# Product 2 of the sequence transform, made once for both pairs of position blocks

## The chip, the core and the metric

The kernel runs on one core of a Trainium2 chip. Its time is device microseconds of that core; lower is better. The engines named below are TensorE (PE; PEld is its weight load), VectorE (DVE), ScalarE (ACT), GpSimd (POOL) and SyncE (SP); SyncE and GpSimd here only issue transfers.

## The reference

The reference mixes two branches of the same kind of input, with S = 2048 positions, D = 512 channels and F = 1792:

```
a = x @ Wd_re.T;  b = x @ Wd_im.T          # DFT along the channels
y = Cr @ a - Ci @ b                        # DFT along the positions, real part
h = relu(x' @ W_gate) * (x' @ W_up);  z = h @ W_down
g = sigmoid(sum(x * gate_w))               # one number per position
out = g * y + (1 - g) * z
```

Cr and Ci are 2048 x 2048 and are loaded from memory as they are used; nothing uses that they are cosines and sines. The change touches y.

## The kernel before, in words

**Products.** Every large product is made on TensorE from two-part numbers: an operand x is split into hi (a ScalarE copy to a shorter format) and lo (VectorE: x minus hi), and three matmuls lo*hi, hi*lo, hi*hi are added in a PSUM bank (PARTS). Every product of matrices is done in Strassen's manner, in Winograd's form: the two matrices are cut into 2 x 2 blocks, seven products of sums of blocks take the place of eight, and the result blocks are sums of these. In this form products 1 (A11*B11) and 2 (A12*B21) add up to result block 11, while the other six make the other three blocks together with product 1.

**Stages.** The hidden layer h (blocks, banks named c), the channel DFT (banks a), then six rounds with banks named z: two of class Down (h times W_down) and four of class Sequence, which make y. A result tile holds channels on the partitions and positions along the free dimension; out, zd have the layout (block of 512 positions, 128 partitions, 4 blocks of 128 channels, 512 positions).

**A round of y** (classes Round, line 779, and Sequence, line 901). A round belongs to one matrix (m = 0 for Cr, m = 1 for Ci) and one pair of 512-position blocks (p = 0 or 1); their order is (0,0), (0,1), (1,1), (1,0). Each of its seven products x has four steps jj, and a step has 2 result tiles x 2 pieces x 3 matmuls = 12 matmuls with 512 columns; so a product has 48 and a round 336. The moving operand (ch and cl, 128 x 1024 for a step) comes from blocks r11, r12, r22, r21 of Cr or Ci: loads by SyncE of 512 KB each (keyed 90 matmuls ahead of the product), sums on VectorE (40 ahead), hi on ScalarE (HI = 31 ahead) and lo on VectorE (LO = 24 ahead). The stationary operand (lh, ll for m = 0; lb, stored earlier and fetched again, for m = 1) is the split of a or b.

Products 1 and 2 go to one pair of banks A, 3 to E, 5 and 6 to B, 7 and 4 to D. After products 6, 2 and 4 the banks are read (evac, line 830): VectorE forms the result blocks 12, 22, 21 with the help of the copies u, n5 and w, and ScalarE copies 11. For m = 0 a result block is added to zd by an accumulating transfer, which GpSimd issues (done, line 962). For m = 1, zd is added to the block by an accumulating transfer, VectorE multiplies by g, and another accumulating transfer adds it to out. The last round has its own order (product 3 first), starts some banks from zd or out with ScalarE copies, and halves its very last step into two half banks (ze) of 256 columns, so that two engines can read and store them at the end.

**What sets the order.** The lines above do not issue instructions: they hand operations with a key (a position in the row of matmuls) to class Plan (line 129). Plan keeps TensorE's order by key and gives every other operation a due time, from which each engine's order follows. It takes an operation at the earliest 70 matmuls ahead of its key on VectorE and ScalarE (AHEAD 40 and FREE 30), 30 ahead on the queues of SyncE and GpSimd, and only when one of 51 working buffers of 4 KB a partition (UNITS) is to be had. The result is one fixed order for each engine; each engine carries out its own strictly in that order.

## Time and profile before

| what | us |
|---|---|
| median of 3 runs (lowest 794.5, highest 795.7) | 795.22 |
| the profiled execution, its own time | 794.13 |
| its span, first to last instruction | 792.4 |
| busy: PE, DVE, ACT, POOL | 787.1, 652.1, 332.6, 97.0 |
| granted TensorE clock, mean | 1.000 |

The profile shows one execution. Its span is 1.7 us shorter than the execution's time, since it counts from the first instruction to the last. A matmul is shown with its own length of some 389 ns, though the next one starts before it ends; so what a matmul costs is read from how many follow each other in a stretch without a gap, not from its mean. An entry such as `cl<-r,ch 128x1024` names what is written and what is read, with the size for 128 partitions; buffer numbers are left out. DMA rows give queue q1 (issued by SyncE), q0 (by GpSimd, the accumulating ones among them), with packets, MB and the share of the 16 DMA engines' time. An arrow in square brackets names what ended the wait in front of the instruction.

### The profile page before, as it was taken

How to read it: one execution, taken by the hardware profiler on the slowest of the kernel's cores; microseconds unless marked ns; L12 is line 12 of the kernel's file. 1: busy time of each engine (PE TensorE's matmuls, PEld its weight loads, DVE VectorE, ACT ScalarE, POOL GpSimd, SP SyncE). 2: the span in 40 equal slices, each digit the busy share in tenths (PEclk: the TensorE clock that was granted, in tenths of full speed). 3: DMA queues.
4: the chain of work that ended last, by engine and by line, in shares of the span. 5: the costliest groups of instructions: out<-in, count | busy, mean ns of one | idle time of the engine just before them, and what ended most of it. 6: DMA issues, size and time to landing. Idle time of an engine off the chain costs nothing.

```text
span 792.4 us, 9557 instructions
## 1 busy us (share of the span) xinstructions
PE 787.1 (99%) x3470; PEld 651.5 (82%) x3470; DVE 652.1 (82%) x778; ACT 332.6 (42%) x402; POOL 97.0 (12%) x151
## 2 busy tenths in 40 slices
PE   9999999999999999999999999999999999999997
PEld 7888888888888888888888888888888888888886
DVE  7999986868699466999886799997597549966996
ACT  5533221312133234274665668464343335442631
POOL 0101311111112122111121001001000100011001
PEclk9999999999999999999999999999999999999999
DMA  8614553232548599999899989217877994098766
GB/s 320 250 41 164 180 187 146 93 147 94 199 146 267 194 353 398 416 349 342 296 367 415 411 285 371 87 53 223 259 271 282 282 379 132 31 278 253 199 147 133
DMA packets 53888, 187.02 MB, mean 236 GB/s; under 512 B 6225, under 2 KB 6993, under 8 KB 53841
## 3 DMA queue, kind: packets, MB, share of 16 engines
q1 hardware_dynamic: 33680, 113.40, 39.9%
q0 software_dynamic: 20016, 72.89, 28.1%
q8 instruction: 27, 0.44, 0.2%
q14 instruction: 21, 0.16, 0.1%
q10 hardware_dynamic: 144, 0.13, 0.1%
HBM read 117.18 MB, written 69.21 MB: 235 GB/s over the span
## 4 chain that ended last, share of the span: by engine, by line
PE 99%; ACT 0%; DVE 0%; issue 0%
PE z L126 55%; PE c L126 34%; PE a L126 10%; PE warm L126 0%; PE ze L126 0%; ACT z L126 0%; DVE warm L126 0%
## 5 line engine op out<-in xcount | busy, mean ns | idle before, releaser
L126 ACT CAST ch<-r 128x1024 fp32r<-128x1024 f32 x112 | 116.0, 1052 | 132.4 <-DVE r L126 54.0
L126 PE MATMUL z<-cl,lh 128*128 128x512 f32 x420 | 163.4, 389 | 0.0
L126 PE MATMUL z<-ch,lh 128*128 128x512 f32 x420 | 163.4, 389 | 0.0
L126 PE MATMUL z<-ch,ll 128*128 128x512 f32 x420 | 163.4, 389 | 0.0
L126 DVE TENSOR_TENSOR cl<-r,ch 128x1024 fp32r<-128x1024 f32 x112 | 134.3, 1218 | 30.9 <-ACT ch L126 22.3
L126 PE MATMUL z<-ch,lb 128*128 128x512 f32 x444 | 136.8, 389 | 0.0
L126 PEld LDWEIGHTS z<-ch,lb 128*128 128x128 f32 x444 | 83.3, 188 | 17.3
L126 PEld LDWEIGHTS z<-cl,lh 128*128 128x128 f32 x420 | 78.8, 188 | 16.5
L126 PEld LDWEIGHTS z<-ch,lh 128*128 128x128 f32 x420 | 78.8, 188 | 16.3
L126 PEld LDWEIGHTS z<-ch,ll 128*128 128x128 f32 x420 | 78.8, 188 | 16.2
L126 PE MATMUL z<-cl,lb 128*128 128x512 f32 x222 | 86.4, 389 | 0.0
L126 DVE TENSOR_TENSOR r<-r,r 128x1024 f32<-128x1024 f32 x60 | 71.5, 1216 | 2.8 <-DMA r<-ci 2.5
L126 DVE TENSOR_TENSOR cl<-hr,ch 128x1024 fp32r<-128x1024 f32 (+1 forms) x56 | 59.8, 1085 | 13.2 <-ACT ch L126 11.3
L126 ACT CAST ch<-hr 128x1024 fp32r<-128x1024 f32 (+1 forms) x56 | 51.4, 942 | 27.7 <-DMA hr<-hd 13.2
L126 PEld LDWEIGHTS z<-cl,lb 128*128 128x128 f32 x222 | 41.7, 188 | 8.7
L126 ACT ACTIVATE g<-c 128x512 f32<-128x512 f32 x26 | 15.5, 597 | 62.7 <-PE c L126 62.5
L126 PE MATMUL c<-xl,wb0h 128*128 128x512 f32 x104 | 40.5, 389 | 0.0
L126 PE MATMUL c<-xh,wb0l 128*128 128x512 f32 x104 | 40.5, 389 | 0.0
L126 PE MATMUL c<-xh,wb1h 128*128 128x512 f32 x104 | 40.5, 389 | 0.0
L126 PE MATMUL c<-xh,wb0h 128*128 128x512 f32 x104 | 40.5, 389 | 0.0
L126 PE MATMUL c<-xh,wb1l 128*128 128x512 f32 x104 | 40.5, 389 | 0.0
L126 PE MATMUL c<-xl,wb1h 128*128 128x512 f32 x104 | 40.5, 389 | 0.0
(200 smaller groups left out, 1321.4 us busy)
## 6 DMA issues: line engine op xcount, KB each, us to landing
hr<-hd SPq DMA_DIRECT2D x42, 512.0 KB, 7.1
r<-cr SPq DMA_DIRECT2D x32, 512.0 KB, 4.8
r<-ci SPq DMA_DIRECT2D x32, 512.0 KB, 8.9
hd<-hs POOLq DMA_DIRECT2D x28, 512.0 KB, 4.7
lb<-lb SPq DMA_DIRECT2D x28, 512.0 KB, 4.7
ad<-a POOLq DMA_DIRECT2D x16, 512.0 KB, 6.0
l<-ad SPq DMA_DIRECT2D x16, 512.0 KB, 8.8
wr<-wgu SPq DMA_DIRECT2D x14, 512.0 KB, 6.5
```

The lines of the kernel that those rows point to most:

```text
L126: getattr(getattr(nc, self.engine), self.name)(*map(ap, self.a), **{k: ap(x) for k, x in self.k.items()})
```

## The change

Product 2 leaves the four rounds. Each round keeps six products in the order 1, 7, 6, 3, 5, 4 (288 matmuls), and result block 11 of a round is product 1 alone. After the two rounds of a matrix a new class Joint makes what is missing: A12 times B21 for both pairs p at once. With the two pairs side by side this is again a product of 2 x 2 blocks, and it is made by seven smaller products with 12 matmuls each (84 in all, one result tile for each bank). Its stationary operands jt are made in Joint.lefts from the stored ad, split, stored to a new place jb and fetched again; its moving operands jch and jcl come from four more blocks of Cr or Ci (jr). Its four result tiles are added to zd (m = 0) or gated and added to out (m = 1). The joint part of m = 1 is the last work of the kernel, and its last product is the one that is halved.

In the rounds the use of the banks changes: after product 1 ScalarE writes its negative into bank B, on which 6 and then 5 are added; after product 6 ScalarE copies the negative of B to u, VectorE subtracts D, and ScalarE starts bank G from u for product 4. Three of the four rounds add r21 to r11 by an accumulating load instead of a load and a VectorE sum. u is completed with zd for m = 1 before it goes into bank G, so block 21 needs no accumulating transfer after it. The keys of the fetches of lb and of the preparations of lefts[0] move with the new order.

The core of the diff, in its order:

```diff
     class Sequence(Round):
+        ORDER, NEW, FOUR = (1, 7, 6, 3, 5, 4), (1, 3, 7), "G"
         HI, LO = 31, 24
...
-                r = {b: buf(f"r{b}") for b in BLOCKS}
-                for b, key in (("11", at[1, jj]), ("22", at[3, jj]), ("12", at[5, jj]), ("21", at[2, jj] - 36)):
-                    op(key - 90, lambda r=r, b=b, jj=jj: load(r[b].all, source(b, jj)))
...
+                for b, x, t in (("11", 1, 90), ("12", 7, 110), ("22", 7, 105)):
+                    op(at[x, jj] - t, lambda r=r, b=b, jj=jj: load(r[b].all, source(b, jj)))
+                for x, o, a, b, sign in ((7, "12", "12", "22", 1), (6, "11", "11", "12", 1), (5, "12", "11", "22", -1)):
+                    op(at[x, jj] - 40, lambda r=r, o=o, a=a, b=b, sign=sign: combine(r[o].all, r[a].all, r[b].all, sign))
+                if self.fourth:
+                    op(at[5, jj] - 36, lambda r=r, jj=jj: accumulate(r["11"].all, source("21", jj)))
+                else:
+                    r["21"] = buf("r21")
+                    op(at[4, jj] - 90, lambda r=r, jj=jj: load(r["21"].all, source("21", jj)))
+                    op(at[4, jj] - 40, lambda r=r: combine(r["11"].all, r["11"].all, r["21"].all, 1))
...
+            def seed():
+                b.new()
+                for n in range(2):
+                    minus(b[n], a[n])
+            def seed4():
+                g.new()
+                for n in range(2):
+                    copy(g[n], u[:, n])
+            if x == 1:
+                op(key, seed)
+                op(key + 1, lambda: both(copy, o["11"], a))
+                self.done("11", key + 6)
+            elif x == 6:
+                op(key, lambda: both(minus, u, b))
+                op(key + 1, lambda: [E().vector.tensor_sub(u[:, n], u[:, n], d[n]) for n in range(2)])
+                if self.m:
+                    op(key + 6, lambda: accumulate(u.all, zd[self.place("21")]))
+                op(key + 50, seed4)
+            elif x == 5:
+                o["12"] = w
+                op(key, lambda: both(copy, w, b))
+                op(key + 1, lambda: both(E().vector.tensor_add, o["22"], d, w))
...
+    class Joint:
+        ORDER = (1, 7, 6, 5, 2, 4, 3)
+        def __init__(self, m, last=False):
+            self.m, self.last, self.base, self.lead = m, last, plan.now, 130 if last else 85
...
+                for p in range(2):
+                    op(self.base - 60, lambda p=p: load(self.v[p].all, out[2 * p, :, 0:2]))
+            for x in self.ORDER:
+                t = self.t[x] = buf(f"jt{x}", [2, 4, P], F32R)
+                op(self.at[x, 0] - 60, lambda t=t, x=x: load(f32(t.all), jb[m, x - 1]))
...
+                if last and x == 3:
+                    for h in range(2):
+                        pe(6, self.halves, h)
+                else:
+                    for jj in range(2):
+                        pe(6, self.product, x, jj)
+                    self.evac(x, plan.now)
...
+        def rights(self, jj):
+            r = {b: buf(f"jr{b}") for b in BLOCKS}
+            at = {x: self.at[x, jj] - self.lead for x in self.ORDER}
...
+            for b, x in (("11", 1), ("12", 1), ("22", 7), ("21", 2)):
+                op(at[x] - 60, lambda b=b: load(r[b].all, source(b)))
...
+                if x == 4:
+                    op(at[6] + 6, lambda: accumulate(r["11"].all, source("21")))
+                if self.last and x == 3:
+                    g = self.g[:, 1].unsqueeze(1).to_broadcast([P, 2, N])
+                    op(at[x] - 3, lambda o=o, g=g: E().vector.tensor_mul(r[o].all, r[o].all, g))
+                hi, lo = self.c[x, jj] = [buf(f"jc{y}{x}", dtype=F32R) for y in "hl"]
+                op(at[x], lambda hi=hi, o=o: E().scalar.copy(hi.all, r[o].all))
+                op(at[x] + 5, lambda hi=hi, lo=lo, o=o: E().vector.tensor_sub(lo.all, r[o].all, f32(hi.all)))
...
+            def seed():
+                self.new("X")
+                e.scalar.activation(bank("X"), bank("A"), AF.Copy, scale=-1.0)
+            def seed3():
+                e.vector.tensor_add(s, bank("B"), s)
+                e.vector.tensor_mul(s, s, self.g[:, 1])
+                e.vector.tensor_add(s, s, self.v[1][:, 0])
+                for n, h in enumerate(HALVES):
+                    self.new(f"H{n}")
+                    e.scalar.copy(self.b[f"H{n}"][:, h], s[:, h])
+            def done(p, n):
+                f = o[p][:, n]
+                e.vector.tensor_mul(f, f, self.g[:, p])
+                e.vector.tensor_add(f, f, self.v[p][:, n])
+                load(out[2 * p, :, n], f)
...
+            if x == 1:
+                op(key, seed)
+            elif x == 6:
+                op(key, lambda: e.scalar.copy(s, bank("X")))
+                op(key + 1, lambda: e.vector.tensor_add(y, bank("D"), s))
...
+    plan.rest = 150
+    for m, k in ((0, 60), (1, 800)):
+        Joint.lefts(m, plan.now + k, 10)
+    plan.rest = plan.REST
     for n, (m, p) in enumerate(((0, 0), (0, 1), (1, 1), (1, 0))):
         if n == 1:
-            for i, x in enumerate(ORDER_Z):
+            for x, key in zip(Sequence.ORDER, (60, 110, 340, 390, 440, 490)):
                 for k in range(2):
-                    lefts[1].fetch(x, k, plan.now + 48 * i + 24 * k + 40, lb)
-        Sequence(lefts[m], m, p, n == 3)
+                    lefts[1].fetch(x, k, plan.now + key + 24 * k, lb)
+        Sequence(lefts[m], m, p, n != 2)
+        if n % 2:
+            Joint(m, m == 1)
```

More of the change, by code (lines that the diff above doesn't have):

```diff
@@ L103, in __init__ @@
             self.reads += self.writes
-        self.after, self.start, self.end, self.due = set(), None, None, None
+        self.after, self.start, self.end, self.due, self.rest = set(), None, None, None, None
         n = writes[0].size() if self.writes else 0
@@ L356, in __getitem__ @@
             return self.banks[n].all
-        def part(self, n, columns):
-            return self.banks[n][:, columns]
     def E():
@@ L796, in __init__ @@
             for x in self.ORDER:
-                self.seed(x, plan.now)
-                self.products(x)
+                for jj, n in enumerate(counts):
+                    pe(6 * n, self.product, x, jj)
                 self.evac(x, plan.now)
@@ L1015, in end @@
[L1015 to L1025 removed]
+            g = self.g[:, int(b[1]) - 1].unsqueeze(1).to_broadcast([P, 2, N])
```

272 lines of the change are left out of this document (141 added, 131 removed).

## The prediction

> **What bounds the kernel now.** I read the chain of work that ended last first. Its rows give start, length and what ran.
>
> ```profile
> 4.49 231.45 PE c L126 x1020
> 235.94 76.16 PE a L126 x336
> 312.10 38.08 PE c L126 x168
> 350.18 436.56 PE z L126 x1926
> 786.74 1.44 PE ze L126 x12
> 788.18 0.02 issue
> 788.20 0.37 ACT z L126
> ```
>
> From 4.49 to 788.18 us the end is set by TensorE alone, with no wait in it. 436.56 us over 1926 matmuls is 0.2267 us for one with 512 columns; 1.44 us over 12 is 0.120 us for one with 256. So time is the number of matmuls, as long as every operand is there in time. The four rounds of y are the last 1344 of these products (1338 with z and 512 columns, 6 split into the 12 of ze): they end at 788.18, and the last one begins 330 x 0.2267 + 1.44 = 76.25 us earlier, at 711.93.
>
> Next, the four rounds one by one (window, PE, PEld, DVE, ACT and POOL busy, clock, DMA share, GB/s), to see what stands close behind TensorE.
>
> ```profile
> 483.40:559.60 76.20, 76.20 (x338) 63.11 (x337) 67.86 (x64) 38.27 (x42) 3.64 (x5) 1.00 0.52 167
> 559.60:635.80 76.20, 76.20 (x338) 63.11 (x337) 55.32 (x52) 30.19 (x33) 3.36 (x4) 1.00 0.84 277
> 635.80:711.90 76.10, 76.10 (x337) 63.01 (x337) 59.84 (x56) 33.48 (x37) 5.16 (x6) 1.00 0.61 199
> 711.90:788.20 76.30, 76.27 (x343) 63.20 (x341) 66.53 (x62) 28.47 (x32) 8.54 (x10) 1.00 0.73 187
> ```
>
> VectorE is busy 55 to 68 of 76 us, the DMA engines 0.52 to 0.84 of the time, ScalarE less than half. The clock is 1.00 throughout. VectorE and the DMA engines are the two to watch.
>
> Third, how far VectorE stands ahead of TensorE, and what eats that lead. These are VectorE's rows around the start of the last round.
>
> ```profile
> 696.15 3.51 DVE L126 TENSOR_TENSOR cl<-r,ch 128x1024 fp32r<-128x1024 f32 x3
> ...
> 721.85 1.23 DVE L126 TENSOR_TENSOR cl<-r,ch 128x1024 fp32r<-128x1024 f32 x1 [2.34 <-ACT ch L126]
> 724.63 1.22 DVE L126 TENSOR_TENSOR r<-r,r 128x1024 f32<-128x1024 f32 x1 [1.55 <-DMA r<-ci]
> 726.79 1.22 DVE L126 TENSOR_TENSOR r<-r,r 128x1024 f32<-128x1024 f32 x1 [0.94 <-DMA r<-ci]
> 727.93 2.48 DVE L126 TENSOR_TENSOR cl<-r,ch 128x1024 fp32r<-128x1024 f32 x2
> ```
>
> By the order of its instructions, the third cl of the first row belongs to the last round's first product: it is done at 699.66, and needed at 711.93, a lead of 12.3 us. The first cl of the last row belongs to the round's third product: done at 727.93 + 1.22 = 729.15, needed 96 matmuls into the round, at 733.69, a lead of 4.5 us. In 30 us VectorE lost 7.8 us, and two of its waits name loads. The DMA rows of that stretch, 696 to 730 us, say why:
>
> ```profile
> q0 software_dynamic: 957, 3.46, 51.0%
> q1 hardware_dynamic: 1843, 6.70, 50.9%
> ```
>
> Both queues together fill all 16 engines for 34 us. So before has no stall, but in its densest 34 us of transfers it used up most of its cover.
>
> **The change part by part.** *Matmuls.* Each round loses one of seven products: 4 x 48 = 192 go. Each of the two joint parts has 7 products x 2 x 6 = 84, so 168 come. Net 24 fewer; and the halved last product makes 24 half matmuls of 12 full ones, where before made 12 of 6. Full matmuls of y: 1338 before, 1152 + 156 = 1308 after, so 30 x 0.2267 = 6.80 us go and 12 x 0.120 = 1.44 us come. **The gain on the path is 5.36 us**, certain as long as nothing waits.
>
> *VectorE.* Its prices, from the trace: one operation, and three in a row.
>
> ```profile
> L126 DVE TENSOR_TENSOR cl<-r,ch 128x1024 fp32r<-128x1024 f32 x112 | 134.3, 1218 | 30.9 <-ACT ch L126 22.3
> 653.47 3.49 DVE L126 TENSOR_TENSOR r<-r,r 128x1024 f32<-128x1024 f32 x3
> 775.51 1.28 DVE L126 TENSOR_TENSOR z<-z,w 128x512 f32<-128x512 f32 x2
> ```
>
> An operation on 1024 columns lasts 1.22 us, but three take 3.49, so the next begins after 1.135 us; on 512 columns after 0.60 (1.28 for two of 0.69). A joint part needs 6 sums and 14 cl, 20 operations on 1024 columns, for 84 matmuls. In the changed order of VectorE, from the fourth round's first cl to the sum that waits for the joint part's product 5, stand 64 operations on 1024 columns and 9 on 512: 64 x 1.135 + 9 x 0.60 = 78.0 us, for 288 + 48 matmuls = 76.2 us. Up to the first cl of product 4, 240 matmuls into that round, it is 48 and 4: 56.9 us and 1.2 for the operation itself, against 54.4 us. VectorE then has no spare time and loses 3.7 us of lead by work alone. The waits that before's last round shows in front of its first dozen operations (2.34, 1.55 and 0.94 us above) are 4.8 us more if they come again. 8.5 us are asked of a lead that was 12.3 at the start of a round and 4.5 at its thinnest: the outcome lies between 3.8 us to spare and 4.0 us late. The nearest row for the state at that point is neither end, since the transfers below are denser than before's; I take **1.8 us late**.
>
> *Transfers.* Prices from the 34 us above, in units of 0.524 MB: accumulating, 0.51 x 34 / (3.46 / 0.524) = 2.62 us; plain, 0.509 x 34 / (6.70 / 0.524) = 1.35 us. From the first load of the first joint part to the end, the changed queues issue 88 plain units (78 full loads and 6 gate rows of half a unit on SyncE, 7 stores of jb on GpSimd) and 29 accumulating ones: 88 x 1.35 + 29 x 2.62 = 195 us. The matmuls of the two joint parts and of rounds three and four last 84 + 288 + 288 full ones and 72 full with 24 half: 149.6 + 19.2 = 168.8 us. The first of these loads are keyed 85 + 60 matmuls ahead, 33 us, so some 192 us stand open (the last 10 us take only results), but the second round's 4 accumulating loads, 10 us, fall into that stretch too. By these prices the engines are 195 + 10 - 192 = 13 us short. A shortage shows first as a loss of VectorE's lead, and the same lead pays for VectorE's own 3.7 us: of 8 to 12 us some 4.3 to 8.6 are left for the transfers, and 4.4 to 8.7 us could reach TensorE. The best that the trace shows is a slice of before with 434 GB/s, 1.21 us for a unit:
>
> ```profile
> GB/s 265 279 275 275 279 270 279 352 410 419 424 410 231 236 284 289 275 275 260 289 289 265 270 260 294 424 270 279 265 265 308 260 279 251 304 410 434 366 313 111
> ```
>
> At that price, with 2.42 for an accumulating one, it is 177 + 10 us: nothing is short. So this part costs 0 to some 9 us. I take **0.7 us** besides the 1.8, near the lower end, because before lived through 34 full microseconds without a stall. The Trainium skill, DMA: Bandwidth & Descriptors, Specifications, gives about 358 GB/s as the limit of HBM for one core. By that rule the 117 units, with the 29 read a second time, would take 146 x 0.524 / 0.358 = 214 us by estimate, and the change would lose some 19 us more than at the prices above; the slices above 400 GB/s here contradict it.
>
> *Banks filled by ScalarE.* Banks X (for product 6 of a joint part) and B are begun with ScalarE copies, and TensorE waits for them. In a round a whole product of 48 matmuls, 10.9 us, lies between; in a joint part only product 7, 12 matmuls, 2.7 us, against one copy of 0.58 us:
>
> ```profile
> L126 ACT COPY u<-z 128x512 f32<-128x512 f32 x8 | 4.6, 584 | 6.1 <-PE z L126 6.1
> z<-zd POOLq DMA_DIRECT2D x5, 512.0 KB, 8.2
> r<-ci POOLq DMA_DIRECT2D x4, 512.0 KB, 9.0
> ```
>
> Queued ahead of that copy on ScalarE is a ch that waits for an accumulating load (9.0 us to landing in the last row). Bounds: nothing, or the 2 to 3 us by which such a ch could be late. I put nothing extra, since it is late only where VectorE is late already.
>
> *The last product.* Its half banks need sums of VectorE after product 5: two of 512 columns, one gating of 1024 that stands between, two more of 512, then a ScalarE copy: 4 x 0.60 + 1.135 + 0.58 = 4.1 us, under products 2 and 4, 24 matmuls, 5.4 us. That holds by 1.3 us, unless the gating waits for its accumulated operand (8.2 us to landing). After product 5 VectorE has 13 operations, 12 x 0.60 + 1.135 = 8.3 us, against 5.44 + 24 x 0.120 = 8.3 us of matmuls: between nothing and half a microsecond of tail, **0.3 us** taken. The rest of the tail (copy, store, 4.2 us from the last matmul to the span's end) keeps its form.
>
> *Sum.* -5.36 + 1.8 + 0.7 + 0.3 = -2.6 us. The profiled execution took 794.13 us (span 792.4 and 1.7 around it), so 791.5; the median of the runs shown, 795.22, lies 1.1 above it: **792.6 us**.
>
> **The rivals.**
> 1. *Nothing waits.* All cover holds, as it does in before, where not one of 3450 matmuls waits. 795.22 - 5.36 = 789.9 us. Against it: VectorE at 78.0 of 76.2 us, where before has 66.5 of 76.3.
> 2. *The transfers become the bound* (the other side). 29 accumulating units where before's last two rounds issue some 16, and 14 stores and loads of jb for each joint part that before has not. It decides from the point where the shortage less the lead that is left exceeds 5.36 us, that is, when a transfer costs the 1.35 and 2.62 us throughout; at the 8.7 us above: 795.22 - 5.36 + 8.7 = 798.6 us. For it: two queues at 102% over 34 us already. Against it: that stretch still cost no matmul.
> 3. *VectorE's lateness just eats the gain*: the 4.0 us end of its bound with 1 to 2 us from the banks of the joint part, 795 us, within 0.2% of before.
> 4. That the change does not do what it says is excluded: the changed program has 3452 matmuls, 24 of them half, for 3470 with 12.
>
> **How the numbers follow.** A measurement of this kernel can tell about 0.2%, 1.6 us, from no change, so faster means under 793.6 and slower over 796.8. Forecast (1 to 3.8 us lost) 0.42, rival 1 0.18, rival 3 0.16, rival 2 0.24. Faster 0.60, same 0.16, slower 0.24. The range starts at rival 1 with the scatter of the runs (lowest 794.5, 0.7 under the median), 789.2, and reaches just past rival 2's time, to 799.0; I leave some 0.06 below and 0.12 above.
>
> **What would show it.** Right: 24 fewer full-width matmuls' time in z and j together, short waits of TensorE on cl near the third product or later of the fourth round, VectorE busy over nine tenths of the last 80 us, a DMA share near 1.0 in the third round. Wrong: no wait of TensorE at all (then the cover was underrated), or waits on loads already in the third round that add up to over 5 us (then the transfers decide), or waits of product 6 of a joint part on ScalarE. What I could have wrong above all is the lead at the start of the fourth round, which I took from before.

## The result, and the profile after

The changed kernel takes **803.77 us** (median; 803.62 to 804.83) beside 794.97 us of the kernel before in the same runs: 1.0113 times as long, with a 95% interval of 1.0095 to 1.013. The forecast was 792.6 us, and its range ended at 799.0. The profiled execution took 803.78 us.

The page of the changed kernel, its span and its engines (busy time, share, instructions):

```profile
span 802.0 us, 9737 instructions
...
PE 787.2 (98%) x3452; PEld 646.7 (81%) x3452; DVE 671.8 (84%) x810; ACT 361.0 (45%) x452; POOL 118.8 (15%) x180
```

There are 3452 matmuls, as the change says. A busy time of 787.2 us for fewer matmuls than before means nothing, since a matmul that waits in the pipeline is shown longer. What counts is the distance from one start to the next. The chain of work that ended last, in order of time (start, length, what ran; the largest pieces of the last six rounds and the joint parts):

```profile
350.81 133.50 PE z L126 x589
...
532.46 14.91 DMA r<-cr
...
549.80 35.27 PE z L126 x155
585.07 15.47 DMA jr<-cr
...
618.08 2.79 PE z L126 x11
...
625.90 15.60 DMA r<-ci
641.51 15.12 DMA r<-ci
...
660.35 27.27 PE z L126 x119
...
695.87 21.33 DMA r<-ci
...
761.55 10.57 DMA jr<-ci
...
794.57 2.88 PE jH L126 x24
```

Up to 484 us the chain is TensorE without a break, as before. Then it leaves TensorE several times, and each time it goes back to a transfer of 11 to 21 us: in the first round, in the second, about the end of the first joint part, at the end of the third round and in the fourth. The same by stage (window, busy PE, PEld, DVE, ACT and POOL, clock, DMA share, GB/s); the windows are the first round, the second, the first joint part, the third round, the fourth, and the last joint part:

```profile
483.90:552.50 68.60, 66.28 (x290) 53.93 (x289) 59.73 (x62) 38.27 (x47) 11.04 (x16) 1.00 0.75 240
552.50:620.70 68.20, 66.43 (x289) 53.71 (x288) 56.53 (x53) 39.10 (x46) 8.47 (x10) 1.00 0.89 260
620.70:639.70 19.00, 19.00 (x85) 15.76 (x84) 13.84 (x14) 6.83 (x10) 1.70 (x2) 1.00 1.01 315
639.70:706.50 66.80, 65.89 (x290) 54.00 (x290) 58.58 (x60) 33.68 (x42) 8.94 (x13) 1.00 1.04 373
706.50:778.10 71.60, 67.38 (x290) 53.58 (x289) 64.13 (x59) 39.26 (x45) 11.12 (x13) 1.00 0.97 268
778.10:797.40 19.30, 19.30 (x97) 16.33 (x95) 17.73 (x23) 5.14 (x8) 3.41 (x4) 1.00 0.92 193
```

A round is 288 matmuls, 288 x 0.2267 = 65.3 us. So the rounds stand still for 3.3, 2.9, 1.5 and 6.3 us, 14.0 together, and the joint parts (84 x 0.2267 = 19.0 us for the first) not at all. With 5.36 us gained, 0.6 us more ahead of the first round and 0.4 us of tail, the span should grow by 9.6 us: it went from 792.4 to 802.0.

The waits that the profile names for TensorE (us in total, times, the longest) do not say transfers:

```profile
PE z L126 <- DVE cl L126: 7.0, 12, 1.8
PE z L126 <- ACT ch L126: 2.1, 2, 1.5
```

They are the last link only. One step further back stand loads. The transfers of 30 us around the start of the fourth round (690 to 720 us; queue, packets, MB, share; then what was issued, how often, KB, and the median us to landing):

```profile
q1 hardware_dynamic: 1791, 6.52, 54.3%
q0 software_dynamic: 1198, 4.31, 48.7%
...
r<-ci SPq DMA_DIRECT2D x10, 512.0 KB, 19.5
```

In the kernel before, the 34 us around the start of its fourth round (696 to 730 us) had 50.9 and 51.0%, and looked the same by that number. But a full share cannot show how much stands in line behind it. The time to landing can: 19.5 us here, and half of that before:

```profile
r<-ci SPq DMA_DIRECT2D x10, 512.0 KB, 9.8
```

VectorE's rows around that place in the changed kernel (start, length, operation, and in brackets its idle time in front):

```profile
700.49 1.22 DVE L126 TENSOR_TENSOR cl<-r,ch 128x1024 fp32r<-128x1024 f32 x1
...
710.68 2.36 DVE L126 TENSOR_TENSOR cl<-r,ch 128x1024 fp32r<-128x1024 f32 x2 [2.15 <-ACT ch L126]
717.29 2.36 DVE L126 TENSOR_TENSOR r<-r,r 128x1024 f32<-128x1024 f32 x2 [4.25 <-DMA r<-ci]
719.69 1.23 DVE L126 TENSOR_TENSOR cl<-r,ch 128x1024 fp32r<-128x1024 f32 x1
```

By the order of instructions the first row is the fourth round's first cl, done at 701.71 and needed at 706.7: a lead of 5.0 us, where before had 12.3. VectorE then idles 4.25 us for a load, and the cl of the last row is done at 720.92, just when TensorE, which has waited 0.5 us for it, goes on. That load (the chain's row of 695.87) was not issued late, as it would be if no buffer had been free: its key is 105 to 110 matmuls, 24 to 25 us, ahead of a step that without a wait begins at 720.1 us, so it was due at 695 to 696 us.

The first round's stall has a queue in it. GpSimd's rows (start, length, how many transfers were issued, its idle time in front), and TensorE's behind them:

```profile
529.55 1.10 POOL L126 DMA_DIRECT2D jb<-jt  x2 [7.89 <-ACT ch L126]
530.64 0.92 POOL L126 DMA_DIRECT2D r<-cr  x1
531.92 0.55 POOL L126 DMA_DIRECT2D jb<-jt  x1 [0.36 <-issue]
532.46 0.90 POOL L126 DMA_DIRECT2D r<-cr  x1
```

```profile
548.54 0.49 PE L126 MATMUL z<-ch,ll 128*128 128x512 f32 x1 [1.54 <-ACT ch L126]
549.80 0.50 PE L126 MATMUL z<-cl,lh 128*128 128x512 f32 x1 [0.77 <-DVE cl L126]
```

The accumulating loads of r21 (r<-cr) stand behind stores of jb on GpSimd, which carries out its queue in order and had idled 7.89 us before them. The last one is issued at 532.46 and lands 14.91 us later, at 547.4, and then ch, cl and TensorE follow in turn.

### The profile page after: what moved, and what is told of

Its sections match the earlier page's. It is cut to its first block, busy times and chain, and to the rows that moved or that the text cites. A ratio compares the mean times of both kernels' runs of the same rounds, so it can differ in the third digit from the quotient of the medians.

```text
span 802.0 us, 9737 instructions
## 1 busy us (share of the span) xinstructions
PE 787.2 (98%) x3452; PEld 646.7 (81%) x3452; DVE 671.8 (84%) x810; ACT 361.0 (45%) x452; POOL 118.8 (15%) x180
## 4 chain that ended last, share of the span: by engine, by line
PE 75%; DMA 12%; DVE 8%; issue 3%; ACT 1%; POOL 0%; DVEq 0%; ACTq 0%; POOLq 0%
PE c L126 34%; PE z L126 29%; PE a L126 9%; DMA r<-ci 6%; DVE cl L126 3%; DMA jr<-cr 2%; DMA r<-cr 2%; DVE r L126 2%; DMA jr<-ci 1%; DVE jr L126 1%; PE jA L126 1%; ACT ch L126 1%; DVE jcl L126 1%; PE jD L126 1%; DVE jt L126 0%
## 5 line engine op out<-in xcount | busy, mean ns | idle before, releaser
L126 PE MATMUL z<-cl,lh 128*128 128x512 f32 x388 | 151.7, 391 | 2.6 <-DVE cl L126 2.5
L126 PE MATMUL z<-ch,ll 128*128 128x512 f32 x388 | 151.1, 389 | 1.5 <-ACT ch L126 1.5
L126 PE MATMUL z<-ch,lh 128*128 128x512 f32 x388 | 151.0, 389 | 0.0
L126 ACT CAST ch<-r 128x1024 fp32r<-128x1024 f32 x96 | 98.1, 1049 | 84.9 <-DVE r L126 50.5
L126 DVE TENSOR_TENSOR cl<-r,ch 128x1024 fp32r<-128x1024 f32 x96 | 115.4, 1221 | 22.7 <-ACT ch L126 22.4
L126 PE MATMUL z<-ch,lb 128*128 128x512 f32 x384 | 119.1, 390 | 0.7 <-ACT ch L126 0.5
L126 PEld LDWEIGHTS z<-ch,lb 128*128 128x128 f32 x384 | 72.1, 188 | 16.4 <-ACT ch L126 1.5
L126 PEld LDWEIGHTS z<-ch,lh 128*128 128x128 f32 x388 | 72.8, 188 | 14.9
L126 PE MATMUL z<-cl,lb 128*128 128x512 f32 x192 | 75.5, 393 | 4.5 <-DVE cl L126 4.5
L126 DVE TENSOR_TENSOR r<-r,r 128x1024 f32<-128x1024 f32 x52 | 62.5, 1220 | 8.8 <-DMA r<-ci 8.8
L126 ACT ACTIVATE g<-c 128x512 f32<-128x512 f32 x26 | 15.5, 597 | 65.8 <-PE c L126 65.8
L126 POOL DMA_DIRECT2D hd<-h x28 | 17.7, 634 | 174.4 <-DVE h L126 174.2
## 6 DMA issues: line engine op xcount, KB each, us to landing
r<-ci SPq DMA_DIRECT2D x28, 512.0 KB, 14.3
```

What stands on the lines that cost most here:

```text
L126: getattr(getattr(nc, self.engine), self.name)(*map(ap, self.a), **{k: ap(x) for k, x in self.k.items()})
```

## The theories

**A: transfers.** The DMA engines have a backlog, loads land late, and what VectorE and TensorE show is the consequence. **B: VectorE.** It has too much work, and the loads would have done. A third reading, **C**, is that a single link is at fault, such as the accumulating load of r21 ahead of product 4. Each has a run or more that takes its own cause away from the changed kernel, and each of A and B one that adds its own cause to the kernel before. The runs named thin_, and no_joint, leave parts of the result out; they show times only.

The table is worked out from the trace of each run: from the first matmul of a stage to the first of the next, less its matmuls at 0.2267 us. So it is the time that TensorE stood still (or ran slower) in that stage. The stalls are those of the one profiled execution, the time in the last column is the median; where a kernel's executions differ much, the two do not belong together (the profiled one of alternate took 795.9 us, of thin_results 795.7, of direct_early_plain 794.5).

| run | round 1 | round 2 | joint 1 | round 3 | round 4 | time, us |
|---|---|---|---|---|---|---|
| the changed kernel | 3.3 | 2.9 | 0 | 1.5 | 6.3 | 803.8 |
| thin_results | 2.1 | 3.0 | 0.1 | 0 | 0 | 796.7 |
| thin_sums | 0 | 0 | 0 | 0.5 | 4.3 | 795.4 |
| thin_both | 0.1 | 0 | 0 | 0 | 0 | 790.5 |
| plain_fourth | 1.1 | 0 | 0 | 2.3 | 8.8 | 805.3 |
| thin_r21 | 0.3 | 0 | 0 | 0 | 6.7 | 797.1 |
| thin_jb | 0.2 | 1.9 | 0 | 0 | 0 | 792.5 |
| thin_lefts | 0 | 2.0 | 0 | 1.5 | 5.6 | 800.1 |
| no_joint | 0.3 | 0 | - | 0 | 0 | 762.8 |
| before_extra1 | 11.6 | 15.1 | - | 24.1 | 12.8 | 861.9 |
| before_extra_half | 3.1 | 1.2 | - | 10.3 | 6.7 | 816.9 |
| before_again | 0.7 | 0 | - | 0 | 9.4 | 804.9 |
| direct_early | 1.6 | 4.6 | 0 | 0 | 0.2 | 796.8 |
| direct_early_plain | 0.4 | 1.0 | 0 | 1.4 | 0 | 793.3 |
| late_fetch | 0 | 0 | 1.9 | 0 | 0 | 793.6 |
| late_fetch_100 | 0 | 1.0 | 0 | 0 | 0 | 792.3 |
| alternate | 0 | 5.1 | 0 | 0 | 0.2 | 798.2 |

The last joint part stood still in none of them.

## The experiments

### Less of one thing in the changed kernel

**thin_results.** In the method that carries an instruction out:

```diff
+        def cut(x):
+            return ap(x)[:, 0:1, 0:128] if isinstance(x, Ref) else x
...
+        f = cut if "accum_op" in self.k and names & {"zd", "out"} else ap
```

> The changed kernel with every instruction in its place; only the accumulating transfers that touch zd or out carry 128 of 1024 columns each, so seven eighths of those sums are left out of the result. Theory A (the DMA engines are full, loads land late, and all other lateness follows): some 28 transfers at 2.62 us become 0.3 us each, over 60 us of engine time go in the four rounds, r<-ci lands in under 10 us again (14.3 in the changed kernel), the stalls of TensorE at the ends of the third round and in the fourth round's product 7 (1.5 and 4.5 us) vanish, and the time comes to 791 to 796 us. Theory B (VectorE's own amount of work is what is late): its 84% stay, the stalls stay, the time stays within 2 us of 803.8.

Measured: 796.72 us (794.83 to 799.72), 1.0023 times before (1.0008 to 1.0039). The waits of TensorE that are left:

```profile
PE z L131 <- DVE cl L131: 2.5, 5, 0.8
...
PE z L131 <- ACT ch L131: 0.7, 1, 0.7
```

r<-ci lands in 9.5 us in place of 14.3, and the third and the fourth round have no stall at all, although VectorE does exactly what it did. There it is the transfers. The stalls of the first and the second round stay (2.1 and 3.0 us, before 3.3 and 2.9), so the result transfers are not their main cause.

**thin_sums.** The same method, with another condition: `f = cut if self.name in ("tensor_add", "tensor_sub") and names <= {r11, r12, r21, r22 and the same with jr} else ap`.

> The changed kernel with every instruction in its place; VectorE's sums of the blocks of Cr and Ci (r and jr) are made on 128 of 1024 columns, so the rest of those sums is left out of the result. Over 50 sums at 1.135 us become some 0.2 us, so VectorE's busy time falls from 671.8 us to about 615 to 620. Theory B (VectorE's own work is the limit): the stalls go, 790 to 793 us. Theory A (loads land late): the wait for the loads is the same, though VectorE makes up for it faster; the stalls that begin with a late load remain, at the least the two at the ends of the first and third rounds and most of product 7 of the fourth, together 6 us or more, 797 to 803 us.

Measured: 795.42 us (793.81 to 797.43), 1.0005 times before (0.9995 to 1.0015). This lies between what the two theories gave, and below what A allowed. The stretch 698.8 to 768.4 us, its fourth round:

```profile
698.80:768.40 69.60, 66.29 (x290) 53.79 (x289) 49.28 (x60) 38.76 (x45) 11.11 (x13) 1.00 1.00 279
```

VectorE is busy 49 of 69.6 us and TensorE still stands for 4.3 us; r<-ci lands in 14.3 us as before. But the first two rounds have no stall, and the others less. A VectorE with time to spare makes good a late load. So A is right on where the stalls of the last two rounds start, and wrong in that VectorE would not matter: its work alone makes the difference between 14.0 and 4.8 us of stalls.

**thin_both.** Both conditions at once.

> Both cuts of the two runs before at once (the same parts of the sums left out). By either theory nearly all stalls go: 789 to 792 us, the changed kernel's number of matmuls without a wait (789.9 us by the prediction's first rival). If it stays above 795, what is late is neither the amount of transfers nor VectorE's work, but the distance between instructions: the accumulating load ahead of product 4 and what follows it in the same step.

Measured: 790.54 us, one run. That is the changed kernel without a wait, and within 0.6 us of the 789.9 us of the prediction's first rival: the gain of 5.36 us is there to be had.

**plain_fourth.**

```diff
-        Sequence(lefts[m], m, p, n != 2)
+        Sequence(lefts[m], m, p, False)
```

> The changed kernel with block r21 loaded plainly and added by VectorE in all four rounds, as in before, in place of three rounds of accumulating loads: 12 accumulating transfers become plain ones (12 x (2.62 - 1.35) = 15 us less engine time) and VectorE gets 12 operations more (12 x 1.135 = 13.6 us). Theory A: fewer stalls, 797 to 801 us, the wait of ch4 in the first round (2.8 us) gone. Theory B: more stalls, 806 to 812 us.

Measured: 805.34 us (804.49 to 806.82), 1.0131 times before (1.0114 to 1.0147); between the two expectations. 15 us less of the engines against 13.6 us more of VectorE moves the stalls (out of the first and second round, into the third and fourth) and takes few away: 12.2 us are left of 14.0, and the end from the last matmul on became 2.7 us longer. The two causes are paid from one account: the lead of the operands, that is, how long before its use VectorE has an operand ready.

**no_joint.** The joint parts and their preparation are taken out of the last loop.

> The changed kernel's four rounds without the joint parts and without the preparation of their stationary operands; product 2 is left out of the result. 168 matmuls and 56 transfers around the joint parts go. Without a stall the time would be 789.9 less 156 x 0.2267 + 24 x 0.120 = 38.2 us, so some 751 to 753 us, the end having no halved product. If the six-product rounds stall by themselves (the accumulating load of r21 ahead of product 4), the 2.8 us at the end of the first round are still there. If what the joint parts add (loads of jr, jt, stores of jb, operations of VectorE) makes the other stalls, then the second, third and fourth round have none, and the time is 752 to 756 us; if the rounds' own transfers make them, 757 to 762 us.

Measured: 762.77 us, one run, above the range. The rounds did as the theory said: 0.3 us of stall in the first, none in the others, and r<-ci lands in 7.9 us. What was wrong is the end: without the joint part nothing covers the last round's results, and 15 us of them follow the last matmul, where the expectation left only a little. So the six-product rounds do not stall by themselves; what the joint parts bring does it.

### Which part of it

**thin_r21.** The cut of thin_results for the accumulating loads into r11 alone.

> The changed kernel with every instruction in its place; the 12 accumulating loads of block r21 into r11 carry 128 of 1024 columns each, the rest of those sums is left out. 12 x 2.62 x 7/8 = 27 us of engine time go, nothing of VectorE's. Were it the landing of this one load that stops product 4, the stalls at the ends of the first and the second round (2.9 and 2.9 us) go, as in plain_fourth, without VectorE's 12 extra sums: 796 to 799 us. Were it VectorE's queue ahead of the load's issue, both stay: 802 to 804 us less what the fourth round gains.

Measured: 797.12 us, one run. The stalls of the first, second and third round go, that of the fourth stays (6.7 us). For the first round C holds: the landing of that load stops product 4, as the rows above show. But the load by itself is not enough, since no_joint has it too and loses 0.3 us; it lands late where the stores of jb stand ahead of it.

In the second round it is not the load's own landing. By the changed kernel's trace the last of these loads has landed there at 599.2 us, and the first cl of product 4 begins at 606.52. What is late are the loads jr of the joint part, whose sums stand ahead of product 4's last cl in VectorE's fixed order (the chain's row of 585.07). In the changed kernel, and then in this run:

```profile
jr<-cr SPq DMA_DIRECT2D x8, 512.0 KB, 13.7
```

```profile
jr<-cr SPq DMA_DIRECT2D x8, 512.0 KB, 6.2
```

So there the accumulating loads cost by the engines' time that they take (27 us less of it in this run), as in A. In the fourth round they are not the cause. The third has none, and why its 1.5 us went too this run does not show.

**thin_jb.** The cut for the stores to jb and the fetches of jt, to one of eight pieces.

```diff
-                    mm(self.b[k][:, columns], self.t[x][:, a, 2 * jj + i], c[b][:, i, columns],
+                    mm(self.b[k][:, columns], self.t[x][:, 0, 0], c[b][:, i, columns],
```

> The changed kernel with every instruction in its place; the 14 stores to jb and the 14 fetches of jt carry one eighth of the bytes, and every matmul of a joint part reads the one piece of jt that is there, so product 2 is not computed rightly. 28 x 1.35 x 7/8 = 33 us of engine time go, spread over the first round, the first joint part, the third round and the last joint part. If it is the way over jb that fills the engines in the third and the fourth round: their stalls (7.6 us) shrink to 2 or less, 796 to 799 us. If the accumulating transfers alone do it: 801 to 804 us.

Measured: 792.51 us, one run; better than either reading expected. The chain from the second round's end on:

```profile
614.38 2.79 PE z L131 x11
617.17 2.72 PE jA L131 x12
...
636.21 130.56 PE z L131 x576
```

576 matmuls of the third and fourth round in 130.56 us, 0.2267 us each: no wait. Its transfers over the whole run, and those of the changed kernel:

```profile
r<-ci SPq DMA_DIRECT2D x28, 512.0 KB, 8.1
...
jb<-jt POOLq DMA_DIRECT2D x14, 64.0 KB, 5.3
jt<-jb SPq DMA_DIRECT2D x14, 64.0 KB, 5.4
```

```profile
r<-ci SPq DMA_DIRECT2D x28, 512.0 KB, 14.3
...
jb<-jt POOLq DMA_DIRECT2D x14, 512.0 KB, 9.9
jt<-jb SPq DMA_DIRECT2D x14, 512.0 KB, 10.2
```

33 us less of the engines' time give back 11.3 us; what thin_results took away was nearly twice as much (26 accumulating transfers, 26 x 2.62 x 7/8 = 60 us) and gave back 7.1. Both free the third and the fourth round; the difference lies in the first two. So it is not the sum of the bytes alone that decides but where they stand. In the first round it is the stores in front of the accumulating loads on GpSimd, as the rows above show. In the third round seven stores, issued from 672.23 to 693.20 us, stand among the loads of r, where the engines are full; which of the transfers there weighs most is not shown.

**thin_lefts.** VectorE's operations that write jt are cut to 64 columns, and a store to jb carries the hi half twice.

> The changed kernel with every instruction in its place; VectorE's 14 operations that make the lo halves of jt work on 64 of 512 columns, and the stores to jb carry the hi half twice (the same bytes) and so do not wait for them; product 2 loses its smallest terms. 14 x 0.5 = 7 us of VectorE's work go, half of it in the first round, half in the third. If VectorE's work for the joint operands makes the first round's stall (2.9 us), it goes, 799 to 801 us; if not, 802 to 804 us.

Measured: 800.07 us, one run. The first round's stall goes, as expected of VectorE's work (or of stores that no longer wait for it: the run cannot tell the two apart), and most of the others stay. Some 1.7 us of its fourth round are matmuls at half clock (see the last section).

### More of one thing in the kernel before

**before_extra1.** In the method that carries an instruction out, after each load into r11, r12, r21 or r22:

```diff
+                t = EXTRA["t"][EXTRA["n"] // 1 % 4]
+                nc.gpsimd.dma_start(out=t[:], in_=ap(self.a[1]))
```

> The kernel before, with the same instructions, and beside each of the 64 loads of a block of Cr or Ci in the four rounds one more copy of the same 512 KB from memory to memory on GpSimd's queue, which nothing waits for. It adds transfers only, no work on VectorE, TensorE or ScalarE: 64 x 1.35 = 86 us of the 16 engines, 0.28 of each round, so that the rounds have 0.80, 1.12, 0.89 and 1.01 of them asked for, about what the changed kernel asks in its last two (1.03 and 0.97). Theory A (full DMA engines alone stop TensorE): loads land in 12 us or more, TensorE waits, 798 to 806 us. Theory B (it takes VectorE's added work too): no stall, 794.5 to 796 us.

Measured: 861.94 us, one run, far beyond both. A copy had to wait for the one four before it, and GpSimd's accumulating transfers stood behind it, so this is not transfers alone. **before_extra_half** is the cleaner form: half the copies, 32 places.

> The kernel before, and beside every second of the 64 loads of a block of Cr or Ci one more copy of the same 512 KB from memory to memory on GpSimd's queue, each to a place of its own, so that GpSimd never waits for one (in before_extra1 a copy waited for the fourth copy before it, and the accumulating transfers behind it on GpSimd waited with it). By the price of a plain transfer, 32 x 1.35 = 43 us of the engines, 0.14 of each round: 0.66, 0.98, 0.75 and 0.87 asked for, nowhere more than there is. By the price that before_extra1 shows for a copy that reads and writes memory, about twice that. Theory A: at the plain price no stall or one in the second round, 795 to 797 us; at twice the price stalls as in the changed kernel or worse, 798 to 815 us, again at operands whose load landed late. Theory B: 794.5 to 796 us.

Measured: 816.94 us, one run. GpSimd's queue was busy 32.5% of 815.0 us where before has 28.1% of 792.4: 42.2 us for 32 copies, 1.32 us each (85 us for the 64 of before_extra1, 1.33 each). The plain price of 1.35 holds, then; that a copy would cost about twice as much, as the expectation says, is wrong; and by the plain price no round has too much. Nevertheless r<-ci lands in 16.0 us and TensorE loses 21.3 us (some of it at half clock, see the last section). Averaged over a round the engines were not full (0.62, 0.91, 0.68 and 0.81 by the trace); in the 39 us ahead of the third round's large stall and the 26 us about the fourth's first they were (1.03 and 1.04). So the balance over long stretches, which this expectation used as the prediction did, is not what decides. (GpSimd issues copies in a row when nothing holds it, which makes the places fuller than the 64 or 32 copies would be evenly.)

**before_again.**

```diff
+        if self.name == "tensor_sub" and self.writes[0].base.name[:2] == "cl" and self.reads[0].base.name[:2] in ("r1", "r2"):
+            AGAIN["n"] += 1
+            if AGAIN["n"] % 5 == 0:
+                nc.vector.tensor_sub(*map(ap, self.a))
```

> The kernel before, with every fifth of the 112 operations that write cl in the rounds carried out twice on VectorE (22 times 1.135 us, 25 us more work there, as much as the changed kernel gives VectorE more in its rounds and joint parts); no transfer is added, the result is the same. VectorE's busy time in the four rounds rises from 68, 55, 60 and 67 us to about 74, 62, 66 and 73 of 76. Theory A (transfers alone): no stall, 794.5 to 796 us. Theory B (VectorE alone): stalls of several us in the first and the fourth round, 798 to 803 us. If the two share one cover, as thin_results and thin_sums suggest: 795 to 798 us, short waits at the thinnest places.

Measured: 804.9 us, one run; more than any expectation. r<-cr lands in 4.5 us, and yet 10 us are lost, 9.4 of them in the fourth round, at one place:

```profile
778.78 0.39 PE L129 MATMUL z<-ch,lb 128*128 128x512 f32 x1
785.43 0.80 PE L129 MATMUL z<-ch,lb 128*128 128x512 f32 x1 [6.26 <-ACT z L129]
```

A bank of the last round is begun by a ScalarE copy from a tile that VectorE had not finished. So B is right as well, in the other kernel: before has no cover for 25 us more of VectorE's work either. Neither VectorE nor the DMA engines may be called the one bound: both have only the lead of the operands and banks between them and TensorE.

### Versions

**direct_early.**

```diff
-    for m, k in ((0, 60), (1, 800)):
+    for m, k in ((1, 60),):
...
+            if not last:
+                self.t = self.lefts(m, self.base - 100, 10)
```

> The changed kernel with the joint part's stationary operands of m = 0 made 100 matmuls ahead and used directly (7 stores and 7 loads of jb less, VectorE's work for them moved from the first round to the second), and those of m = 1 made in the first round in place of the third. Theory A: the third round loses 7 stores and 2 loads at 1.35 us, 12 us, the stretch about the first joint part 7 loads, 9.5 us; the stalls of the third and fourth round (7.6 us) shrink to 3 us or less, 794 to 799 us. Theory B: VectorE has 9 more operations of half a unit in the second round, its stall there (2.9 us) grows to 5 or more, 801 to 806 us.

Measured: 796.81 us (795.46 to 798.70), 1.003 times before (1.0016 to 1.0044). The time is A's, and the third and fourth round have 0.2 us left of 7.8. The growth that B expected in the second round came nearly as large, to 4.6 us; its cause is followed up under alternate.

**direct_early_plain.** Besides, `Sequence(lefts[m], m, p, n not in (0, 1, 2))`.

> The run before (direct_early), and besides block r21 loaded plainly and added by VectorE in the first two rounds too, so that only the fourth still accumulates. By the run plain_fourth this takes the stalls of the first and the second round away (2.8 and 2.9 us), since product 4 waits for no accumulating load there. If the two effects add up: 790 to 795 us, faster than before. If VectorE's extra sums bring back what they save, 796 to 801 us.

Measured: 793.28 us (791.82 to 796.14), 0.9985 times before (0.9974 to 0.9996). The effects add up nearly. (What the plain loads change in the second round is told under alternate; it is not that product 4 waits for the accumulating ones.)

**late_fetch.** Besides, the keys (340, 390, 440, 490) of the fetches of lb become (370, 420, 470, 520), and the lead of 100 becomes 85.

> direct_early_plain with two keys moved: the fetches of lb for products 6, 3, 5 and 4 of the third round start 30 matmuls (6.8 us) later, since they land 24 us and more ahead of their use and stand in front of the third round's loads of Ci on SyncE's queue; and the operands of the first joint part are made 85 matmuls ahead in place of 100. Theory A: the third round's stall at product 7 (1.4 us) goes, the one at the end of the second round (0.9 us) stays or goes: 790.5 to 793 us. If the order of the loads is not what counts there, 793 to 795 us as before the move.

Measured: 793.55 us (791.89 to 794.67), 0.998 times before (0.9969 to 0.9991). The third round's stall went, as A said, though the number of transfers is the same (the next run, with the lead of 100, shows that the moved keys did it); a new one came in the first joint part, where the last operations on jt stand in front of a bank's read on VectorE.

**late_fetch_100.** late_fetch with the lead of 100 kept.

> late_fetch with the operands of the first joint part made 100 matmuls ahead, as in direct_early_plain, in place of 85. The stall of the first joint part (1.6 us, a bank's read by VectorE behind the last operations on jt) goes; cl4 at the end of the second round stands 0.7 us ahead in VectorE's order in place of 1.8, so that up to 1 us can come there: 791 to 793.5 us.

Measured: **792.28 us** (791.36 to 793.59), 0.9967 times before (0.9955 to 0.9979). This is 2.7 us, a third of a percent, under the kernel before, and well under the changed one. Its third and fourth round:

```profile
634.80:700.10 65.30, 65.30 (x289) 54.08 (x289) 56.02 (x53) 32.20 (x37) 5.96 (x7) 1.00 1.03 354
700.10:765.40 65.30, 65.30 (x289) 54.07 (x288) 61.76 (x56) 37.20 (x43) 11.20 (x13) 1.00 0.96 250
```

The DMA shares are 1.03 and 0.96, in the changed kernel 1.04 and 0.97, and VectorE is busy 95% of the fourth round; and nothing waits. In the 30 us around the start of that round (684 to 714 us):

```profile
r<-ci SPq DMA_DIRECT2D x8, 512.0 KB, 6.6
```

6.6 us to landing where the changed kernel had 19.5 (the share in these 30 us is 0.95 beside 1.03). So neither a full DMA share nor a busy VectorE is a stall. Nor is a late landing by itself: around the start of the third round of this same kernel eight loads r<-ci, issued from 618 to 630 us, landed after 17.4 us at the median, and no matmul of the third round waited; VectorE's results stood 0.5 us ahead of their use at the thinnest. A stall comes where the line in front of a load is longer than the lead that is left at its place.

**alternate.** late_fetch with `n not in (0, 2)` and a lead of 120.

> late_fetch with block r21 accumulated in the second round too (plain in the first and the third), and the operands of the first joint part made 120 matmuls ahead: by the order of VectorE's instructions cl4 at the end of the second round stands 3.9 us ahead of its use in place of 1.8. If the order of VectorE decides there: 790.5 to 793 us. If the landing of the accumulating loads decides, as in direct_early, a stall of 2 to 4 us comes back at the end of the second round: 794 to 797 us.

Measured: 798.23 us (794.70 to 801.47), 1.0039 times before (1.0025 to 1.0053). That VectorE's order alone decides at the end of the second round has fallen: it was the better order, and 5.1 us are lost there. But product 4 does not wait for the accumulating loads themselves either, as the expectation has it: the last one has landed at 594.8 us, and the first cl of product 4 begins at 603.07. Beside them the loads jr<-cr, whose sums VectorE has ahead of the later cl, land after 15.5 us at the median. In late_fetch_100, which loads r21 plainly, they land after 7.2 us, and the same place costs 1.0.

What stays open: whether in the first round the stores of jb or VectorE's operations for them weigh more, since thin_jb and thin_lefts each take that stall away; which of the transfers of the third round weigh most; and what the runs with a single time would give with an interval (one kernel's executions lie up to 6.8 us apart, in alternate).

## Why the prediction was wrong, point by point

- **The gain on the path, 5.36 us: right.** thin_both comes to 790.5 us beside 789.9, and late_fetch_100 keeps half of it, 2.7 us.
- **Banks filled by ScalarE, nothing; the halved last product; the tail of 0.3 us: right.** Neither joint part of the changed kernel has a wait, and the time from the last matmul to the end grew by 0.4 us, to 4.6.
- **Transfers, taken at 0.7 us: this step failed.** In the stretch that this term covers, from the first loads of the joint part on, TensorE lost 10.7 us (2.9, 1.5 and 6.3 in the second, third and fourth round). The third and fourth round's share of that is 7.8 us, and thin_jb, thin_results and late_fetch_100, which take transfers out of that stretch or out of the loads' way, lose nothing there; the second round's 2.9 us go with seven eighths of the r21 loads' bytes (thin_r21). The prediction's own working gave 4.4 to 8.7 us; it left it because "before lived through 34 full microseconds without a stall". But before lived through them on 7.8 us of lead that it had, and a full share told nothing of the line behind it (loads landed in 9.8 us then, in 19.5 after the change). The signs were in the change itself: the jb and jt transfers go to the two queues that carry the accumulating loads and r.
- **The stretch over which transfers were balanced: too late and too long.** It began with the first joint part's loads. The first round, 3.3 us of the 14.0, was given no price at all, though the stores of jb start there. And a balance over 192 us cannot see places; before_extra_half stalls with no round over its means.
- **VectorE, 1.8 us late: right in kind, not as a term of its own.** Its rivalry with the transfers for one lead was said, and thin_sums, before_again and plain_fourth show it. But 95% busy without a wait in late_fetch_100 shows that the 78.0 us for 76.2 were not the trouble. The late end of its bound, 4.0 us, also charged the three waits twice: the 4.5 us from which it took them is what was left after them.
- **The lead at the start of the fourth round, 12.3 us, named as the weakest point: it was.** It was 5.0 us; the third round began with 8.1 us and ended with 4.0. And the 4.5 us "at its thinnest" was read in the last round alone. Worked out in the same way for every step (the n-th cl of VectorE against the n-th step's first matmul that reads cl), before's lead falls to 1.8 us in the first round, 2.1 us in the third and 4.1 us in the fourth. So the round that was given no price had the least cover. The code also holds VectorE closer than the description of Plan says: FREE counts only in the last 200 matmuls, so that elsewhere an operation is planned at most 40 matmuls, 9.1 us, ahead of its key.
- **The rivals.** Rival 2 comes nearest: its price of 8.7 us stands against 10.7 us in its stretch, and 3.3 us came from the first round. The argument against it, that before's stretch cost no matmul, is the one that failed. But transfers alone are not the bound, since thin_sums takes 9.2 of the 14.0 us away with all transfers in place. The sign "waits on loads already in the third round that add up to over 5 us" did not come so: that round lost 1.5 us, TensorE names cl and ch, and the loads stand one link behind; the largest stall, in the fourth, goes back to a load issued in the third. And three of the signs of being right came although the forecast failed (short waits on cl in the fourth round, VectorE busy 77.7 of the last 80 us of matmuls, a DMA share of 1.04 in the third round): they did not tell the forecast from rival 2. Of before, "not one of 3450 matmuls waits" should read 3462, the sum of the chain's rows; it holds.
- **The Trainium skill's limit** of about 358 GB/s for one core (DMA: Bandwidth & Descriptors, Specifications), which the prediction set aside, stays contradicted: the third round moved 373 GB/s over 66.8 us.

## What to carry to other kernels

When two engines and the transfers share one lead, a change that adds a little to each is priced by the lead that is left at each place, not by what each has to spare on average. Read a load's time from issue to landing, and what stands ahead of it on its queue: a DMA share of 1.0 does not tell how long that line is, and a long landing time is harmless only where the load was issued that much earlier. And where operands go by way of memory only to be kept, ask whether making them later or earlier costs less than the way.

## What the runs showed of the hardware that was not expected

A long wait of TensorE costs more than itself. In before_extra1 (starts of matmuls, idle time in front; then windows as above):

```profile
595.93 0.50 PE L129 MATMUL z<-ch,ll 128*128 128x512 f32 x1 [1.60 <-ACT ch L129]
607.24 0.80 PE L129 MATMUL z<-cl,lh 128*128 128x512 f32 x1 [10.81 <-DVE cl L129]
607.83 0.63 PE L129 MATMUL z<-ch,lh 128*128 128x512 f32 x1
608.26 0.63 PE L129 MATMUL z<-ch,ll 128*128 128x512 f32 x1
```

```profile
585.00:593.00 8.00, 8.00 (x37) 6.63 (x36) 2.45 (x2) 2.10 (x2) 0.49 (x1) 1.00 1.09 376
...
608.00:612.00 4.00, 4.00 (x12) 3.09 (x11) 4.00 (x5) 1.05 (x1) 0.00 (x0) 0.52 1.02 418
```

For some 4 us after the wait the granted clock is 0.52 and matmuls start 0.43 us apart in place of 0.2267, about 2 us lost. In all the traces here every wait of 3.2 us or more (start to start, less 0.2267) is followed by this; the longest that is not is 3.0 us (direct_early). But length does not decide alone: one wait of 2.8 us was enough (before_extra1, at 521.94), and in rows of shorter waits 2.1 us (thin_lefts) and 1.1 us (before_extra_half, at 751.13) were. In before_again the wait of 6.4 us brings 2.4 us more. The Trainium skill, TensorE: Matmul & The Clock Gate, What's actually happening, says that the clock is halved after an idle window of about 3.4 us until about as long of activity. These traces agree in the length of the halved stretch, 3.4 us or a multiple of it in the clock's records, but not in the wait that it takes: 2.8 us of waiting, and rows of waits of about 1 us, had the same effect. The changed kernel's waits, 1.8 us at most by the profile, bring nothing of the kind: its clock is 1.00 in every stage.

Two prices were not as expected. An accumulating load of 0.5 MB, which the planner takes to land 4.1 us after the engines have moved it, lands 9.3 (r<-cr) and 10.4 us (r<-ci) after its issue at the median of the changed kernel, and 14.9 us in the first round, where the engines were full (1.03 from 530 to 548 us). And a copy from memory to memory costs the DMA engines no more than a load: 1.32 us beside 1.35.
